# Local attention in blocks of 32 queries by 64 keys, in strips of TensorE, with two heads to a transpose and a bank for one head of two pairs

## The chip, the cores and the metric

The kernel runs on one core of a Trainium2 chip. The metric is the device time of one execution in microseconds (us). Five engines work side by side and meet at semaphores: TensorE (PE; its weight loads are shown apart as PEld), VectorE (DVE), ScalarE (ACT), GpSimd (POOL), and SyncE (SP), which here only issues DMAs. Matmul results land in PSUM, which has 8 banks of 128 partitions by 512 floats.

## The reference

Three layers follow each other on 4 sequences of 576 positions; 8 heads of 64 make a model width of 512.

```python
# q, k, v: (4, 8, 576, 64), float32
scores = scale * np.matmul(q, k.transpose(0, 1, 3, 2))
rel = pos[:, None] - pos[None, :]
mask_local = (rel >= 0) & (rel < 32)                                # heads 0 to 3
mask_strided = (rel >= 0) & (pos[None, :] % 32 == pos[:, None] % 32)  # heads 4 to 7
scores = np.where(masks, scores, -1e9)
attn = np.exp(scores - max); attn = attn / (sum + 1e-09); out = attn @ v
x = out as (2304, 512)
h = np.maximum(np.maximum(x @ w1, x @ w2), x @ w3); x = h @ w_out    # width 768
h = x @ w_in; g = np.maximum(h, 0) + alpha * np.minimum(h, 0); out = g @ w_out2  # width 2048
```

A query of a local head sees its own position and the 31 before it, so a block of 32 queries needs the 64 keys of its own block and of the block before.

## The kernel before

Every large product is split: a float32 number is held as two float32r parts (high and low), and three matmuls make the product. These matmuls leave one record in the trace each. The matmuls of the attention take plain float32 operands; each stands once in the program and leaves two records in the trace, a weight load and a matmul twice. A transpose (a matmul by the identity) leaves one.

The program has three stages. In the first, a planner (class Weave, lines 50 to 162) weaves together four kinds of tasks: the attention of all four sequences, the conversion of the weights (they arrive as float64 words; ACT and DVE make float32 of them, and cut that in two), the first layer's products for the first three sequences (gate_products, line 617; out1_products, line 639), and sums of weights for later. Each task has an engine, a cost in ns, a position that says how early it is wanted, and the tasks and buffers that it needs; the planner walks through time with these costs and writes down the order in which each engine gets its instructions. So the order is fixed when the kernel is built, and a change of a cost or a task moves others too. In the second stage the first layer runs for the last sequence, in the third the second layer runs for all (lines 1222, 1023 and 1029).

The attention is done in units: a sequence b, a pair of heads cc (0 and 1 are local, 2 and 3 strided; a pair lies in the 128 partitions of q and k, one head j in each 64), and a half hf of the sequence (288 positions). For a local unit there are 3 tiles of 96 queries by 128 keys, and for both heads:

- scores (line 331): 6 matmuls, each contracting 64 rows; head j writes its own bank.
- masked (line 339, DVE): adds the mask, scales, and takes the row minimum, per tile and head.
- exponential (line 346, ACT): exp with a row sum, per tile and head; then DVE takes reciprocals.
- normalise (line 368 on ACT or line 370 on DVE, as the planner chooses): per head, 3 tiles of 128 keys.
- transposes (line 378): 3 per head into a bank per head; keep (line 266 on ACT or DVE) copies the bank to a tile pt.
- values (line 403): 6 matmuls; head j writes 64 partitions of one bank; the result is split into x (a cast on ACT, a difference on DVE at line 269), the input of the first layer.

There are 16 local units, 4 per sequence, and 16 strided ones. The units of the first sequence come before any product can start; until then TensorE fills gaps with 38 matmuls whose results nobody reads (unread, line 215). A product of the first layer needs x of all four pairs of its half, and one converted weight tile. The weight tile's last two steps are a cast on ACT (line 266, "w<-word") and a difference on DVE (line 269, "w<-word,w").

```python
for i, (_, _, t, _) in enumerate(tiles):          # values, before
    for j in range(2):
        nc.tensor.matmul(pv[D * j:D * (j + 1), nq * i:nq * (i + 1)], v[:nk, t, j, :],
                         tl["pt", u, j][:nk, nq * i:nq * (i + 1)], start=True, stop=True)
```

Of the kernel before, what the change touches and what calls it, by code (L numbers as in the profile page):

```python
# [10 lines left out]
F32 = mybir.dt.float32  # L11
# [19 lines left out]
KT = 128  # L31
# [15 lines left out]
X_SPLIT = 10  # L47

# [117 lines left out]
def attention_maxout_prelu_kernel(  # L166
# [20 lines left out]
    mask_l = const.tile([QT, KT], F32, name="mask_l")  # L187
    mask_l0 = const.tile([QT, KT], F32, name="mask_l0")
# [3 lines left out]
    def build_constants():  # L192
# [4 lines left out]
        for m in (mask_l0, mask_l):  # L197
            g.memset(m, 0.0)
            g.affine_select(out=m, in_=m, compare_op=ALU.is_ge, fill=BIG, base=32,
                            pattern=[[-1, KT]], channel_multiplier=1)  # L200
            g.affine_select(out=m, in_=m, compare_op=ALU.is_ge, fill=BIG, base=-1,
                            pattern=[[1, KT]], channel_multiplier=-1)
        g.affine_select(out=mask_l0, in_=mask_l0, compare_op=ALU.is_ge, fill=BIG, base=-32,
                        pattern=[[1, KT]], channel_multiplier=0)
# [5 lines left out]
                        pattern=[[NA, 7], [0, NA]], channel_multiplier=-1)  # L210

# [35 lines left out]
    vp = pool(ax, "vp", 2)  # L247
# [13 lines left out]
    weave = Weave({"bank": 8, "q": 2, "third q": 1, "v": 2, "e": 3, "pt": 4, "x": 11, "t": 4, "h": 12,  # L261
# [19 lines left out]
    def geometry(cc, hf):  # L281

        if cc < 2:
            return QT, KT, [(QT * t, QT * t, t, mask_l0 if t == 0 else mask_l)
                            for t in range(3 * hf, 3 * hf + 3)]
# [6 lines left out]
    def load_task(b, cc, pos):  # L292
# [12 lines left out]
        def emit_v(_):  # L305
            v = tl[vk] = vp.tile([P, 6 if cc < 2 else 5, 2, D], F32, tag="v", name="v")
            nc.sync.dma_start(v, vl[b, cc] if cc < 2 else vs[b, cc - 2])

        add(load(592), emit_qk, pos, gives=[qk], makes=[("third q" if third else "q", qk)])
        add(load(350), emit_v, pos + 1, gives=[vk], makes=[("v", vk)])  # L310

    def attention_tasks(b, cc, hf, pos, step):
# [5 lines left out]
        ek, qk, vk = ("e", u), ("q", b, cc), ("v", b, cc)  # L318
        banks = [("sc", u, j) for j in range(2)]

        def scores(_):
# [3 lines left out]
            tl[ek] = ep.tile([P, 2, 3, KT], F32, tag="e", name="e")  # L325
            for name in ("nm", "sm", "rc"):
                tl[name, u] = smp.tile([P, 2, 3], F32, tag=name, name=name)
            for i, (qo, ko, _, _) in enumerate(tiles):
                for j in range(2):
                    rows = slice(D * j, D * (j + 1))  # L330
                    nc.tensor.matmul(sc[j][:nq, KT * i:KT * i + nk], q[rows, qo:qo + nq],  # L331
                                     k[rows, ko:ko + nk], start=True, stop=True)

        add((("PE", 2 * n * nk),), scores, pos, needs=[qk], gives=[("sc", u)],
            makes=[("bank", key) for key in banks] + [("e", ek)], uses=[qk], mode="scores")
        for i, (_, _, _, m) in enumerate(tiles):
            def masked(_, i=i, m=m):
                for j in range(2):
                    nc.vector.tensor_tensor_reduce(  # L339
                        out=tl[ek][:nq, j, i, :nk], in0=tl["sc", u][j][:nq, KT * i:KT * i + nk],  # L340
# [11 lines left out]
            add((("ACT", 750),), exponential, pos, needs=[("nm", u, i)], gives=[("exp", u)],  # L352
# [8 lines left out]
        for j in range(2):  # L361
            trk, ptk = ("tr", u, j), ("pt", u, j)

            def normalise(engine, j=j):
                e, rc = tl[ek][:nq, j, :n, :nk], tl["rc", u][:nq, j, :n]
                if engine == "ACT":
                    for i in range(n):
                        nc.scalar.activation(e[:, i], e[:, i], AF.Copy, scale=rc[:, i:i + 1])
                else:
                    nc.vector.tensor_tensor(out=e, in0=e, in1=rc.unsqueeze(2).to_broadcast([nq, n, nk]),  # L370
                                            op=ALU.mult)

            def transposes(_, j=j, trk=trk, ptk=ptk):
                tr = tl[trk] = bank()
                unread(tr, UNREAD.get((u, j), 0))
                tl[ptk] = ptp.tile([P, 3 * KT], F32, tag="pt", name="pt")
# [4 lines left out]
            def keep(e, trk=trk, ptk=ptk):  # L381
                copy(e, tl[ptk][:nk, :n * nq], tl[trk][:nk, :n * nq])

            add((dve(n * nk), ("ACT", n * (140 + 5 * nk // 6))), normalise, pos, needs=[("rc", u)],
                gives=[("nrm", u, j)], uses=[ek])
# [5 lines left out]
        pvk = ("pv", u)  # L391
        halves = [hf] if cc < 2 else [0, 1]
        xks = [("x", b, cc, h) for h in halves]
        fresh = [k for k in xks if k not in weave.users]

        def values(_):
# [3 lines left out]
            v = tl[vk]  # L400
# [7 lines left out]
            needs=[vk] + [("pt", u, j) for j in range(2)] + ([begun] if cc >= 2 and hf else []),  # L408
            gives=[pvk] + ([begun] if cc >= 2 and not hf else []), makes=[("bank", pvk)] + [("x", k) for k in fresh],
            uses=[vk] + [("pt", u, j) for j in range(2)] + xks, mode="values", slack=slack)  # L410

        def parts(h):
            x, pv = xt[b, cc, h], tl[pvk]
            if cc < 2:
                return x[:, 0, :], x[:, 1, :], pv[:, :n * nq]
# [5 lines left out]
        for h in halves:  # L421
            size = n * nq // len(halves)
            hik = ("xhi", u, h)
# [959 lines left out]
```

## Time and profile before

| | |
|---|---|
| median of 3 runs | 747.36 us (746.64 to 748.55) |
| the profiled execution | 747.21 us, of which its span from the first to the last instruction is 745.4 us |
| PE, PEld busy in the span | 99%, 96% |
| DVE, ACT, POOL busy | 85%, 64%, 4% |
| granted clock of TensorE | 1.000 |

A group line gives the busy time of all its instructions and the mean length of one, from start to end. Matmuls overlap each other, so on PE the length of one says little about the rate; the rate is read from a timeline, where one group's start can be set against the next group's start.

### The profile page before, as it was taken

Reading aid. Unit: us, or ns where it says so; the run is one execution under the profiler, and the core shown is the slowest. Engines: PE = TensorE matmul, PEld = TensorE weight load, DVE = VectorE, ACT = ScalarE, POOL = GpSimd, SP = SyncE. Lnnn points to the kernel's source line nnn. Section 1 sums busy time; section 2 is a strip of 40 time slices with the busy share of each in tenths; the row PEclk is TensorE's granted clock in tenths of the full one; section 3 lists DMA queues with packets and bytes.
Section 4 is the critical chain, followed back from the end, with each engine's and each line's share of the span. In section 5 each row is a group of like instructions: output and inputs, shape, how many; then the busy total and the mean of one; then the engine's idle time right before and its main releaser. Section 6 shows DMA issues by size and latency. Waiting matters only on the chain.

```text
span 745.4 us, 16034 instructions
## 1 busy us (share of the span) xinstructions
PE 736.9 (99%) x5586; PEld 712.7 (96%) x5586; DVE 629.9 (85%) x1684; ACT 475.2 (64%) x1268; POOL 27.6 (4%) x41
## 2 busy tenths in 40 slices
PE   9899999999999999999999999999999999999998
PEld 6699999999999999999999999999999999999997
DVE  5988998899989989558769898888989888988896
ACT  7997997779787677332255656624575654556571
POOL 1000000000000000034400000000000000000000
PEclk9999999999999999999999999999999999999999
DMA  8476779987999785579899789999788999877362
GB/s 302 132 231 211 252 257 318 357 313 267 316 323 352 266 271 201 172 278 336 279 323 389 270 296 333 381 397 384 250 306 302 365 402 370 284 240 265 107 200 75
DMA packets 88928, 211.95 MB, mean 284 GB/s; under 512 B 11024, under 2 KB 41232, under 8 KB 88848
## 3 DMA queue, kind: packets, MB, share of 16 engines
q1 hardware_dynamic: 88848, 210.94, 80.6%
q8 instruction: 44, 0.72, 0.4%
q14 instruction: 36, 0.29, 0.1%
HBM read 154.80 MB, written 56.10 MB: 283 GB/s over the span
## 4 chain that ended last, share of the span: by engine, by line
PE 89%; ACT 3%; DVE 3%; DMA 2%; POOL 2%; issue 1%; SPq 0%; POOLq 0%; ACTq 0%; DVEq 0%
PE bank L617 26%; PE ph L1222 22%; PE po L1023 15%; PE bank L639 10%; PE po L1029 4%; PE ph L1023 3%; PE bank L331 2%; PE bank L403 2%; PE bank L378 2%; PE po L1033 2%; ACT e L346 2%; POOL xst L223 1%; DMA xs<-x 1%; DMA xd<-xst 1%; PE bank L215 1%
## 5 line engine op out<-in xcount | busy, mean ns | idle before, releaser
L1222 PE MATMUL ph<-x,w 128*128 128x384 f32 x990 | 200.2, 337 | 0.2 <-DVE c L1228 0.2
L617 PE MATMUL bank<-x,w 128*128 128x288 f32 x1440 | 197.9, 296 | 1.2 <-DVE w L269 1.2
L617 PEld LDWEIGHTS bank<-x,w 128*128 128x128 f32 x1440 | 191.9, 188 | 3.3 <-DVE w L269 1.4
L1222 PEld LDWEIGHTS ph<-x,w 128*128 128x128 f32 x990 | 166.3, 188 | 1.4 <-DVE c L1228 0.7
L1023 PE MATMUL po<-w,g 128*128 128x256 f32 x936 | 135.6, 281 | 0.0
L1023 PEld LDWEIGHTS po<-w,g 128*128 128x128 f32 x936 | 130.1, 189 | 0.3
L1228 DVE TENSOR_TENSOR c<-ph,c 128x384 f32<-128x384 f32 x165 | 89.4, 554 | 30.3 <-PE ph L1222 27.5
L1016 ACT CAST g<-c 128x384 fp32r<-128x384 f32 x93 | 47.0, 506 | 91.1 <-DVE c L1206 51.7
L639 PE MATMUL bank<-h,w 128*128 128x288 f32 x576 | 79.8, 297 | 0.1
L639 PEld LDWEIGHTS bank<-h,w 128*128 128x128 f32 x576 | 76.9, 188 | 1.3 <-DVE h L777 0.4
L269 DVE TENSOR_TENSOR w<-word,w 128x512 fp32r<-128x512 f32 x100 | 63.4, 641 | 10.5 <-ACT w L266 9.8
L346 ACT ACTIVATE e<-e,nm 96x128 f32<-96x128 f32 (+2 forms) x176 | 68.2, 399 | 6.3 <-DVE nm L339 6.3
L1166 ACT ACTIVATE c<-c 128x384 f32<-128x384 f32 x96 | 50.5, 526 | 32.8 <-DVE c L1228 31.7
L266 ACT CAST w<-word 128x512 fp32r<-128x512 f32 x100 | 57.9, 590 | 12.7 <-DMA wh<-w 4.0
L1167 ACT ACTIVATE c<-c,nalpha 128x384 f32<-128x384 f32 x96 | 59.2, 617 | 3.1
L1171 DVE SCALAR_TENSOR_TENSOR c<-c 128x384 f32<-128x384 f32 x96 | 52.9, 551 | 6.4 <-ACT c L1167 6.4
L1017 DVE TENSOR_TENSOR g<-c,g 128x384 fp32r<-128x384 f32 x96 | 52.8, 550 | 0.9 <-ACT g L1016 0.5
L1017 DVE TENSOR_TENSOR g<-k,g 128x384 fp32r<-128x384 f32 x72 | 36.9, 550 | 7.5 <-ACT g L1016 7.5
L1029 PE MATMUL po<-w,g 128*128 128x512 f32 x120 | 43.0, 398 | 0.0
L469 ACT ACTIVATE word<-raw 128x512 f32<-128x512 f32 x56 | 37.4, 681 | 8.6 <-DMA raw<-in_w 5.0
L1206 DVE TENSOR_TENSOR k<-c 128x384 f32<-128x384 f32 x72 | 37.8, 550 | 0.0
L1016 ACT CAST g<-k 128x384 fp32r<-128x384 f32 x72 | 33.1, 514 | 7.1 <-PE ph L1023 3.3
(109 smaller groups left out, 953.2 us busy)
## 6 DMA issues: line engine op xcount, KB each, us to landing
w<-wh SPq DMA_DIRECT2D x72, 512.0 KB, 5.2
raw<-in_w SPq DMA_DIRECT2D x50, 512.0 KB, 4.8
w<-wo SPq DMA_DIRECT2D x48, 512.0 KB, 6.0
w<-wp SPq DMA_DIRECT2D x36, 512.0 KB, 6.2
wh<-w SPq DMA_DIRECT2D x24, 512.0 KB, 4.6
xd<-xst SPq DMA_DIRECT2D x28, 384.0 KB, 3.3
x<-xd SPq DMA_DIRECT2D x28, 384.0 KB, 8.4
ws<-w SPq DMA_DIRECT2D x12, 512.0 KB, 4.3
```

What stands on the lines that cost most here:

```text
L266: (nc.scalar.copy if e == "ACT" else nc.vector.tensor_copy)(out_, in_)
L269: nc.vector.tensor_tensor(out=out_, in0=x, in1=y, op=ALU.subtract)
L346: nc.scalar.activation(tl[ek][:nq, j, i, :nk], tl[ek][:nq, j, i, :nk], AF.Exp, bias=tl["nm", u][:nq, j, i:i + 1], scale=-1.0, accum_out=tl ...
L617: nc.tensor.matmul(acc, words["gate", f, g][:, wi, cc * P:(cc + 1) * P], xt[b, cc, hf][:, xi, :], start=n == 0, stop=n == 3 * NCC - 1)
L639: nc.tensor.matmul(acc, words["mix", f][:, wi, dc * P:(dc + 1) * P], st["h", hf, f][:, xi, :], start=n == 0, stop=n == 3 * NF1 - 1)
L1016: cast(g[:, 0], x)
L1017: return g, lambda: nc.vector.tensor_tensor(out=g[:, 1], in0=x, in1=g[:, 0].bitcast(F32), op=ALU.subtract)
L1023: nc.tensor.matmul(bank[:, NH * half:NH * (half + 1)], g[:, gi, t * P:(t + 1) * P], w[:, wi, off:off + NH], start=first and i == 0, stop=l ...
L1029: nc.tensor.matmul(bank.rearrange("p (s n) -> p s n", n=NH), g[:, 0, t * P:(t + 1) * P], w[:, :, off:off + NH], start=first, stop=last)
L1167: nc.scalar.activation(a, a, AF.Copy, scale=nalpha[:, f:f + 1])
L1222: nc.tensor.matmul(bank, words["h", n, i][:, wi, off + c * P:off + (c + 1) * P], x2h[blk, k, c][:, xi, :], start=m == 0, stop=m == 5)
L1228: nc.vector.tensor_tensor(out=out_, in0=bank, in1=other, op=ALU.add)
```

## The change

Local units are cut finer. Scores are made for 32 queries by 64 keys: 18 matmuls of 64 columns in a unit in place of 6 of 128, and a matmul's 64 contraction rows and 32 output partitions are those of one strip of TensorE out of six (two heads by three blocks of a tile). The mask and the tiles of scores and exponentials are 64 keys wide instead of 128. Both heads of a tile lie side by side in 128 columns, so normalise is one instruction for both heads on DVE alone, a transpose takes both heads (3 in a unit in place of 6), and one bank and one copy take what two did. The values of the two local pairs of a half are made in one task: 36 matmuls that contract 64 keys, with 64 output partitions and 32 columns, in four quadrants; a bank holds head j of both pairs. So x groups heads 0 and 2, and 1 and 3, and the rows of the first layer's weights are put in that order. The values' operand v is laid out by blocks of 64 keys, so that keys stand twice, and comes in one load per unit with 3 buffers instead of 2. The planner's costs for the new tasks are 500 and 1000 ns.

```diff
-KT = 128
+KW = 64
+NB = S // STRIDE
+COST = (500, 1000)
...
-        for m in (mask_l0, mask_l):
-            g.memset(m, 0.0)
-            g.affine_select(out=m, in_=m, compare_op=ALU.is_ge, fill=BIG, base=32,
-                            pattern=[[-1, KT]], channel_multiplier=1)
...
+        for m in (mask_l0, mask_l):
+            g.memset(m, 0.0)
+            for q in range(0, QT, STRIDE):
+                rows = m[q:q + STRIDE]
+                g.affine_select(out=rows, in_=rows, compare_op=ALU.is_ge, fill=BIG, base=STRIDE,
+                                pattern=[[-1, KW]], channel_multiplier=1)
+                g.affine_select(out=rows, in_=rows, compare_op=ALU.is_ge, fill=BIG, base=-1,
+                                pattern=[[1, KW]], channel_multiplier=-1)
...
-    vp = pool(ax, "vp", 2)
+    vp = pool(ax, "vp", 3)
...
+            if cc < 2:
+                for i, (qo, _, _, _) in enumerate(tiles):
+                    for o in range(0, QT, STRIDE):
+                        for j in range(2):
+                            rows = slice(D * j, D * (j + 1))
+                            nc.tensor.matmul(sc[j][o:o + STRIDE, KW * i:KW * (i + 1)],
+                                             q[rows, qo + o:qo + o + STRIDE],
+                                             k[rows, qo + o:qo + o + KW], start=True, stop=True)
+                return
...
-        add((("PE", 2 * n * nk),), scores, pos, needs=[qk], gives=[("sc", u)],
+        add((("PE", COST[0] if cc < 2 else 2 * n * nk),), scores, pos, needs=[qk], gives=[("sc", u)],
...
-        for j in range(2):
+        heads = [(0, 1)] if cc < 2 else [(0,), (1,)]
+        for js in heads:
...
+                elif len(js) == 2:
+                    nc.vector.tensor_tensor(out=e, in0=e, in1=rc.unsqueeze(3).to_broadcast([nq, 2, n, nk]),
+                                            op=ALU.mult)
...
                 for i in range(n):
-                    nc.tensor.transpose(tr[:nk, nq * i:nq * (i + 1)], tl[ek][:nq, j, i, :nk],
-                                        ident[:nq, :nq])
+                    e = (tl[ek][:nq, j, i, :nk] if len(js) == 1 else
+                         tl["whole e", u][:nq, rows * i:rows * (i + 1)])
+                    nc.tensor.transpose(tr[:rows, nq * i:nq * (i + 1)], e, ident[:nq, :nq])
...
+    def local_values(b, hf, pos, slack):
...
+            for t in range(NB // 2):
+                cols = slice(STRIDE * t, STRIDE * (t + 1))
+                for cc in range(2):
+                    for j in range(2):
+                        rows = slice(D * j, D * (j + 1))
+                        nc.tensor.matmul(tl[pvs[j]][D * cc:D * (cc + 1), cols],
+                                         tl[vks[cc]][rows, D * t:D * (t + 1)], tl[pts[cc]][rows, cols],
+                                         start=True, stop=True)
+
+        add((("PE", COST[1]),), values, pos, needs=vks + pts, gives=pvs,
...
+            if cc < 2:
+                values_task(("v", b, cc, hf), vl[b, cc, hf], first + step * i - 7)
...
-    vl = np.stack([vpad[:, :, QT * t:QT * t + KT] for t in range(6)], axis=2)
+    vl = np.stack([vpad[:, :, STRIDE * t:STRIDE * t + KW] for t in range(NB)], axis=3)
...
+    w1 = np.stack([moe_w1, moe_w2, moe_w3]).reshape(3, H, D, F1)[:, [0, 2, 1, 3, 4, 5, 6, 7]]
```

The order of PE's instructions in the second sequence's attention, among the first sequence's products (L617 and L639 before, L682 and L704 after). Before, from a group of transposes to the values of the sequence's last local units:

```order
L378 MATMUL bank<-ident,e 128x96 x6
L331 MATMUL bank<-k,q 96x128 x6
L639 MATMUL bank<-h,w 128x288 x36
L617 MATMUL bank<-x,w 128x288 x36
L331 MATMUL bank<-k,q 108x108 x6
L403 MATMUL bank<-pt,v 64x96 x12
L378 MATMUL bank<-ident,e 128x96 x12
L639 MATMUL bank<-h,w 128x288 x18
L403 MATMUL bank<-pt,v 64x96 x12
```

The same place in the changed kernel (L346 are the local scores, L408 the transposes, L483 the local values):

```order
L408 MATMUL bank<-ident,e 128x96 x3
L346 MATMUL bank<-k,q 32x64 x18
L704 MATMUL bank<-h,w 128x288 x18
L408 MATMUL bank<-ident,e 128x96 x3
L704 MATMUL bank<-h,w 128x288 x18
L682 MATMUL bank<-x,w 128x288 x36
L408 MATMUL bank<-ident,e 128x96 x3
L483 MATMUL bank<-pt,v 64x32 x36
```

Six score matmuls have become 18, six transposes three, and twelve value matmuls 36; they still stand between products.

PE's order where the first products begin, at the end of the first sequence's attention. Before:

```order
L378 MATMUL bank<-ident,e 128x96 x6
L331 MATMUL bank<-k,q 96x128 x6
L403 MATMUL bank<-pt,v 64x96 x6
L215 MATMUL bank<-warm_r 128x512 x9
L378 MATMUL bank<-ident,e 128x96 x6
L331 MATMUL bank<-k,q 108x108 x6
L403 MATMUL bank<-pt,v 64x96 x6
L378 MATMUL bank<-ident,e 128x96 x6
L331 MATMUL bank<-k,q 126x126 x4
L403 MATMUL bank<-pt,v 64x96 x6
L617 MATMUL bank<-x,w 128x288 x240
```

After, from the same 9 unread matmuls:

```order
L218 MATMUL bank<-warm_r 128x512 x9
L408 MATMUL bank<-ident,e 128x96 x3
L353 MATMUL bank<-k,q 108x108 x6
L483 MATMUL bank<-pt,v 64x32 x36
L408 MATMUL bank<-ident,e 128x96 x3
L353 MATMUL bank<-k,q 126x126 x4
L682 MATMUL bank<-x,w 128x288 x12
L408 MATMUL bank<-ident,e 128x96 x3
L682 MATMUL bank<-x,w 128x288 x12
L483 MATMUL bank<-pt,v 64x32 x36
L682 MATMUL bank<-x,w 128x288 x216
```

Two products (12 matmuls each) now stand ahead of the second half's values, where all of them stood behind.

ACT's order in the same stretch, from the last exponentials of the first sequence's local units to the third cast of a weight ("w<-word"). Before:

```order
L266 COPY pt<-bank 128x288
L368 ACTIVATE e<-e,rc 96x128 x3
L478 ACTIVATE raw<-raw 128x512
L266 CAST x<-bank 128x288
L266 COPY pt<-bank 128x288 x2
L469 ACTIVATE word<-raw 128x512
L346 ACTIVATE e,sm<-e,nm 108x108 x2
L266 CAST x<-bank 128x288
L266 COPY pt<-bank 128x288
L346 ACTIVATE e,sm<-e,nm 108x108 x2
L478 ACTIVATE raw<-raw 128x512
L266 CAST w<-word 128x512
```

After, from the copy of the first local unit's transposes (L368 are the exponentials here, L534 and L543 steps of the weights' conversion):

```order
L269 COPY pt<-bank 128x288
L368 ACTIVATE e,sm<-e,nm 96x64 x4
L269 CAST w<-word 128x512
L368 ACTIVATE e,sm<-e,nm 96x64 x6
L269 CAST w<-word 128x512
L269 CAST x<-bank 128x288 x2
L269 COPY pt<-bank 128x288
L534 ACTIVATE word<-raw 128x512 x3
L543 ACTIVATE raw<-raw 128x512 x3
L269 COPY pt<-bank 128x288
L769 COPY t<-bank 128x288
L269 CAST w<-word 128x512 x3
```

The first weight cast has moved ahead of the last local exponentials and the second right behind them; the exponentials of the next sequence's strided units (108x108) have moved behind five casts; the normalise on ACT is gone. Before, three instructions stand between the first and the second cast (two exponentials among them), and six exponentials between the second and the third.

## Rows read from the trace of the kernel before

**Rows 1.** The page: span, busy time of PE, clock in 40 slices (tenths).

```profile
span 745.4 us, 16034 instructions
PE   9899999999999999999999999999999999999998
PEclk9999999999999999999999999999999999999999
```

**Rows 2.** Busy time of each engine (instructions) in two stretches, clock, DMA share, GB/s.

```profile
20.00:37.00 17.00, 14.13 (x156) 10.50 (x152) 15.62 (x89) 17.00 (x74) 0.00 (x0) 1.00 0.44 138
37.00:313.00 276.00, 276.00 (x2355) 267.03 (x2356) 244.18 (x748) 217.71 (x661) 0.00 (x0) 1.00 0.81 276
```

**Rows 3.** The chain that ended last: the piece that follows the first stretch.

```profile
36.99 31.79 PE bank L617 x238
```

**Rows 4.** PE's timeline around a local unit's scores: start, length, records.

```profile
89.30 0.90 PE L331 MATMUL bank<-k,q 64*96 64x128 f32 x12
90.13 0.78 PE L403 MATMUL bank<-pt,v 108*64 108x108 f32 x12
```

**Rows 5.** PE's timeline: values and transposes of two local units, then products.

```profile
114.98 1.21 PE L403 MATMUL bank<-pt,v 128*64 128x96 f32 x24
116.12 1.21 PE L378 MATMUL bank<-ident,e 96*128 96x96 f32 x12
117.12 2.66 PE L639 MATMUL bank<-h,w 128*128 128x288 f32 x18
```

**Rows 6.** Weight loads by shape over the run: busy, mean ns of one.

```profile
L617 PEld LDWEIGHTS bank<-x,w 128*128 128x128 f32 x1440 | 191.9, 188 | 3.3 <-DVE w L269 1.4
...
L403 PEld LDWEIGHTS bank<-pt,v 128*64 128x64 f32 x192 | 8.8, 136 | 2.3 <-ACT pt L266 1.0 <-issue 0.7
```

**Rows 7.** PE's timeline where the first products begin.

```profile
34.41 0.95 PE L403 MATMUL bank<-pt,v 128*64 128x96 f32 x12
35.29 0.53 PE L617 MATMUL bank<-x,w 128*128 128x288 f32 x2
36.99 3.23 PE L617 MATMUL bank<-x,w 128*128 128x288 f32 x22 [1.17 <-DVE w L269]
```

**Rows 8.** ACT's timeline before and at the first weight casts.

```profile
29.11 0.99 ACT L368 ACTIVATE e<-e,rc 96x128 f32<-96x128 f32 x3
30.00 0.67 ACT L478 ACTIVATE raw<-raw 128x512 uint32<-128x512 uint8 x1
...
34.62 0.62 ACT L266 CAST w<-word 128x512 fp32r<-128x512 f32 x1
...
38.96 0.62 ACT L266 CAST w<-word 128x512 fp32r<-128x512 f32 x1
```

**Rows 9.** Groups of ACT and DVE by shape over the run: busy, mean ns.

```profile
L346 ACT ACTIVATE e<-e,nm 96x128 f32<-96x128 f32 x96 | 37.7, 405 | 1.8 <-DVE nm L339 1.8
...
L346 ACT ACTIVATE e<-e,nm 108x108 f32<-108x108 f32 x48 | 18.0, 384 | 4.5 <-DVE nm L339 4.5
...
L368 ACT ACTIVATE e<-e,rc 96x128 f32<-96x128 f32 x36 | 11.9, 405 | 0.6 <-DVE rc L358 0.6
...
L266 ACT COPY pt<-bank 128x288 f32<-128x288 f32 x29 | 10.0, 411 | 0.0
...
L339 DVE CUSTOM_DVE_ANT_0 e<-bank,mask_l 96x128 f32<-96x128 f32 x96 | 21.4, 282 | 0.5 <-PE bank L331 0.4
...
L339 DVE CUSTOM_DVE_ANT_0 e<-bank,mask_s 108x108 f32<-108x108 f32 x48 | 9.7, 264 | 6.0 <-PE bank L331 6.0
...
L370 DVE TENSOR_TENSOR e<-e,rc 96x384 f32<-96x384 f32 x20 | 10.6, 547 | 0.0
```

**Rows 10.** POOL's groups: one of the mask's instructions, busy, mean ns.

```profile
L199 POOL TENSOR_SCALAR_AFFINE_SELECT mask_l<-mask_l 96x128 f32<-96x128 f32 x2 | 0.6, 289 | 0.1
```

**Rows 11.** DVE's timeline: the first use of a local mask.

```profile
15.53 0.28 DVE L339 CUSTOM_DVE_ANT_0 e<-bank,mask_l 96x128 f32<-96x128 f32 x1
```

**Rows 12.** DMA issues: number, KB each, median us to landing.

```profile
v<-in_vl SPq DMA_DIRECT2D x8, 384.0 KB, 3.8
```

More of the change, by code (lines that the diff above doesn't have):

```diff
@@ L283, in geometry @@
         if cc < 2:
[L284 removed]
+            return QT, KW, [(QT * t, QT * t, t, mask_l0 if t == 0 else mask_l)
                             for t in range(3 * hf, 3 * hf + 3)]
@@ L303, in emit_qk, with values_task, emit @@
             tl[qk] = q, k
-        def emit_v(_):
-            v = tl[vk] = vp.tile([P, 6 if cc < 2 else 5, 2, D], F32, tag="v", name="v")
-            nc.sync.dma_start(v, vl[b, cc] if cc < 2 else vs[b, cc - 2])
         add(load(592), emit_qk, pos, gives=[qk], makes=[("third q" if third else "q", qk)])
-        add(load(350), emit_v, pos + 1, gives=[vk], makes=[("v", vk)])
+        if cc >= 2:
+            values_task(vk, vs[b, cc - 2], pos + 1)
+    def values_task(vk, src, pos):
+        def emit(_):
+            tl[vk] = vp.tile([P, 10 * D], F32, tag="v", name="v")
+            n = src.shape[1]
+            nc.sync.dma_start(tl[vk][:, :n], src)
+        add(load(src.shape[1] // 2), emit, pos, gives=[vk], makes=[("v", vk)])
     def attention_tasks(b, cc, hf, pos, step):
@@ L351, in attention_tasks @@
                 uses=banks + [ek])
-            add((("ACT", 750),), exponential, pos, needs=[("nm", u, i)], gives=[("exp", u)],
+            add((("ACT", 640 if cc < 2 else 750),), exponential, pos, needs=[("nm", u, i)], gives=[("exp", u)],
                 uses=[ek])
@@ L374, in transposes @@
+            def transposes(_, j=j, js=js, trk=trk, ptk=ptk):
                 tr = tl[trk] = bank()
                 unread(tr, UNREAD.get((u, j), 0))
-                tl[ptk] = ptp.tile([P, 3 * KT], F32, tag="pt", name="pt")
+                tl[ptk] = ptp.tile([P, 3 * P], F32, tag="pt", name="pt")
+                rows = nk * len(js)
                 for i in range(n):
-                    nc.tensor.transpose(tr[:nk, nq * i:nq * (i + 1)], tl[ek][:nq, j, i, :nk],
-                                        ident[:nq, :nq])
@@ L386, in attention_tasks, with keep @@
+            def keep(e, js=js, trk=trk, ptk=ptk):
+                rows = nk * len(js)
+                copy(e, tl[ptk][:rows, :n * nq], tl[trk][:rows, :n * nq])
+            add((dve(n * nk * len(js)),) + ((("ACT", n * (140 + 5 * nk // 6)),) if len(js) == 1 else ()),
+                normalise, pos, needs=[("rc", u)], gives=[("nrm", u, j)], uses=[ek])
             add((("PE", 95 * n),), transposes, pos + step, needs=[("nrm", u, j)], gives=[trk],
@@ L389, in attention_tasks @@
                 uses=[trk, ptk])
-        pvk = ("pv", u)
-        halves = [hf] if cc < 2 else [0, 1]
-        xks = [("x", b, cc, h) for h in halves]
+        pts = [("pt", u, js[0]) for js in heads]
+        if cc < 2:
+            if cc == 1:
+                local_values(b, hf, pos + 2 * step, slack)
+            return
+        vk, pvk = ("v", b, cc), ("pv", u)
+        xks = [("x", b, cc, h) for h in (0, 1)]
         fresh = [k for k in xks if k not in weave.users]
@@ L407, in attention_tasks @@
         add((("PE", 2 * n * 85),), values, pos + 2 * step,
-            needs=[vk] + [("pt", u, j) for j in range(2)] + ([begun] if cc >= 2 and hf else []),
-            gives=[pvk] + ([begun] if cc >= 2 and not hf else []), makes=[("bank", pvk)] + [("x", k) for k in fresh],
-            uses=[vk] + [("pt", u, j) for j in range(2)] + xks, mode="values", slack=slack)
+            needs=[vk] + pts + ([begun] if hf else []),
+            gives=[pvk] + ([] if hf else [begun]), makes=[("bank", pvk)] + [("x", k) for k in fresh],
+            uses=[vk] + pts + xks, mode="values", slack=slack)
         def parts(h):
             x, pv = xt[b, cc, h], tl[pvk]
-            if cc < 2:
-                return x[:, 0, :], x[:, 1, :], pv[:, :n * nq]
             r0, nr = RG[tiles[0][2]][0], n * nq // NA
```

74 lines of the change are left out of this document (43 added, 31 removed).

## The prediction

> **What bounds the kernel now.** I read the page first: PE is busy in nearly every slice, and its granted clock is at full speed (2.4 GHz) throughout [rows 1]. Then the stretches: from 37 to 313 us, where the attention of the last three sequences is woven between the first layer's products, PE is busy for all of 276 us, DVE for 244 and ACT for 218 [rows 2]. There PE's own time is the time, and what comes off PE comes off the run. From 20 to 37 us it is ACT that never rests (17.00 of 17.00), while PE has 14.13 busy, part of it matmuls that nobody reads [rows 2]. The chain agrees: from 36.99 us it is PE alone, 238 products in a row [rows 3]. The first product starts at 35.29, waits for a weight's low part from DVE, and PE runs without a gap from 36.99 [rows 7]. So two things can be gained: PE time behind 37 us (12 local units, 6 pairs of them), and an earlier start, which ACT and DVE decide.
>
> **How long local attention takes on PE now.** Starts are compared, since lengths overlap. Scores of a unit: 12 records from 89.30 to 90.13, 0.83 us [rows 4]. Values of two units: 24 records from 114.98 to 116.12, 1.14 us; transposes of two units: 12 records from 116.12 to 117.12, 83 ns each [rows 5]. A transpose passes 96 columns and fills the array: 83 ns is twice 96 columns at 2.4 GHz (80 ns) and 3 ns. A value record passes 96 columns too, but they come every 47.5 ns, although each must last as long: two run side by side, one in each half of the columns. Twelve rounds of 83 ns are 0.99 us, the other 0.15 us goes at the change of shapes. Scores likewise: 128 columns are 107+3 ns, six rounds of two make 0.66, and 0.17 goes at the ends. So I take as rule, from these rows, that a plain float32 record of n columns holds its own strip for 2n/2.4+3 ns, and that different strips work side by side.
>
> The Trainium skill says that tiles of the array load weights and multiply independently, and lists eight of 64x32 and four of 64x64 (TensorEngine Tiling (Array Packing), Tiling Modes). The two-strip rows agree; no row shows more than two at a time.
>
> **The change on PE.** Scores: 36 records of 64 columns in six strips, six rounds of 56 ns, with 0.17 at the ends 0.51 us; I take 0.53, since the last strip of a round starts later. That is 0.30 less a unit, 3.6 us for 12. Transposes: three of 83 ns less, 0.25 a unit, 3.0 us. Values: 72 records of 32 columns in four quadrants, 18 rounds. The columns take 27+3 ns, but each record first needs 64 weight columns: a load of 128 columns takes 188 ns and one of 64 takes 136 [rows 6], so 64 columns cost 52 ns beyond a fixed part. I take 55 ns, 18 rounds 0.99, with the ends 1.14: no gain. (At 30 ns a round, 0.69: another 2.7 us off; that is the bound below.) Sum behind 37 us: 6.6 us. A bound above comes from the fastest rate that a row shows, 47.5 ns from record to record [rows 5]: with s ns between records, twelve times (36s+0.17-0.83 us), six times (72s+0.15-1.14 us) and the transposes' 3.0 make 864s-16.9 us, so -16.9 is what it takes off and s decides. Rounds of 56 for six and 55 for four strips are a mean s of 12. At 47.5 ns it would be 24 us more, at 19.5 ns nothing. I take the side of the concurrent strips, since the rows show the second strip of a pair costing next to nothing.
>
> **The change on ACT and DVE, in the first stretch.** An exponential of 128 columns takes 405 ns and one of 108 takes 384, so 1.05 ns a column: 64 columns less are 67 ns, 24 of them in the first sequence 1.6 us. The three normalise instructions on ACT, 0.99 us there [rows 8], are gone, and five copies of 411 ns (about 0.3 from start to start) become three [rows 9]. That is 3.2 us off an engine that was full. On DVE the mask drops by 0.9 ns a column (282 against 264 ns), 58 ns by 24, 1.4 us; seven normalise instructions (547 ns each; eight heads less the one that ACT did) become four of the same 384 elements, 1.6 us [rows 9]. Beside this the order on ACT changes. Before the third weight cast, which ended at 39.58 [rows 8], stood 12 exponentials of the next sequence's strided units; they go behind it (12 by 0.37 from start to start, 4.4 us), and five more conversion steps come ahead of it (0.67 long [rows 8], about 0.58 from start to start, 2.9 us). With the 3.2 us and 0.5 of small copies that go to DVE or behind, the third cast ends near 39.6-3.2-4.4+2.9-0.5 = 34.4. Products were in step with it before: one takes 12x31.79/238 = 1.60 us [rows 3], so the third was due at 40.2, just behind cast and difference. Now the first two products can start near 30.5, when the pair's x is done, and the third near 35.0. The delayed exponentials come back ahead of the sixth weight: its cast I count at 40.5 and its product from 41.2 to 42.8, against 36.99+6x1.60 = 46.6. I take 3.8 us, with 2 to 6.5 as bounds: 2 where little more than half of the 3.2 us that ACT sheds arrives, 6.5 where products start at 30.5 and never wait.
>
> **What costs nothing.** GpSimd makes 12 selects for the local masks instead of 5; at 289 ns each [rows 10] it is 2 us later, and DVE first reads a local mask at 15.53 us [rows 11], long behind it. Without that cover it would delay the first local unit by 2 us. Values come in 16 loads of 288 KB in place of 8 of 384 [rows 12], 1.5 MB more; in the stretch from 37 us the DMA engines have 19% free at 276 GB/s [rows 2], and 1.5 MB takes some 6 us of 276. One of these loads now stands on SP's queue ahead of the first weight loads; 288 KB is about 1 us at that rate, and the first cast (34.62 [rows 8]) waits for ACT, not for its load. With three buffers in place of two, loads wait less for a free one, and the weights behind them on the queue too. The weights' row order moves no instruction.
>
> **Sum.** The profiled execution took 747.21 us, 1.8 more than its span, and is within 0.2 of the median. 747.2-6.6-3.8 = **736.8 us**. Its own range is 731 to 742: at one end 2.7 us more off in the values and 6.5 at the start, at the other 2 at the start and half of PE's gain.
>
> **Rivals.**
> - *Only two strips at a time* (slower). Whatever lets two records run may not hold six. Then scores take 18 rounds of 56 ns, 1.18 us, and values 36 of 55, 2.13: 12x0.35+6x0.99-3.0 = 7.1 us more; the start keeps some 2 us: 752. For it: no row shows three. Against it: rows show both ways of cutting the array, by rows (scores) and by columns (values), each at work. It decides as soon as the mean spacing is over 24 ns (864s = 16.9+3.8 with the start's gain).
> - *A floor under the spacing of records*, whatever their strips. For it: 47.5 ns is the closest mean that a timeline row has. At 24 ns it just cancels all gains, at 30 it is 5 us slower. Against it: in these rows columns explain the whole time. I price it where it about cancels: 748.
> The Trainium skill states such a floor: start to start never below 25 ns however few the columns (TensorE: Matmul & The Clock Gate, "Wait — 56ns, not 53.3ns?"), and warns against tiling a dimension that is already small (TensorEngine Tiling (Array Packing), Instruction Overhead). If it held across strips, 864x25 ns gives 21.6-16.9 = 4.7 us more on PE, and 748.1 in all. The trace neither bears it out nor refutes it: its closest mean is 47.5 ns.
> - *The strips do not work side by side at all* (the change doesn't do what it says): 36 records at 56 ns are 2.2 us, 72 at 55 are 4.1: 12x1.35+6x3.0-3.0 = 31 us more, 778. Against it: the pairs in today's rows.
> - *The start gives nothing*, since DVE, 15.6 of 17 us busy, holds back the weights: 740.6, still faster.
>
> **How the numbers follow.** Change in both parts as worked out (731 to 742): 0.70, of which the start without gain has 0.08 at its upper end. Two strips at a time 0.09; a floor or slow issue near 748 0.10; no concurrency 0.03; a new wait that I don't see, with a small change either way, 0.08. From no change the runs can tell about 0.3%, 2.2 us: faster (under 745.1) 0.74, same 0.11, slower 0.15. The range of 8 in 10 must take in the rival near 748: 729.5 to 750.
>
> **What would show it.** Six strips: the timeline has 36 records of local scores in about 0.5 us, and 72 of values in about 1.1. If scores take 1.1 or more, one of the slow rivals is right; the values tell which (1.8 times the scores' length for two at a time, twice for a floor). Transposes stand three at a time, 0.25 us. The first products start near 30 us, with a pause before the third, and PE has no gap from about 35. In the stretch to the last product of the first stage, which ended at 313, PE stays full, and the next stage starts 11 us earlier. The forecast is wrong if PE shows gaps behind the start that end on DVE's normalise (now on DVE alone), or if its clock drops in the first stretch, where PE now has less to do.

## The result, and the profile after

The changed kernel takes 738.7 us (median of 4 executions, 737.37 to 738.95) against 747.16 beside it: a ratio of 0.988 (95% interval 0.9862 to 0.9898), 8.5 us faster, where 10.4 were forecast. The profiled execution took 737.37 us, 735.5 of it span, so 9.8 us less than that of before.

The page of the changed kernel: span, PE's share in 40 slices, and its clock in tenths.

```profile
span 735.5 us, 17464 instructions
...
PE   8899999999999999999999999999999999999998
...
PEclk9999999999999999999999999999999999999999
```

Of the 40 slices only the first (18 us) shows PE less full than before [rows 1]. The stretches say where the time came from. First the changed kernel, cut at its first product, the end of its sixth product, the end of its 138th product (114 of 12 matmuls and 24 of 18), and the first product of the last stage; columns as in [rows 2].

```profile
0.00:30.60 30.60, 25.88 (x383) 19.90 (x383) 20.61 (x142) 24.66 (x113) 4.67 (x24) 1.00 0.74 254
30.60:42.50 11.90, 11.59 (x149) 11.05 (x148) 11.27 (x32) 11.90 (x36) 0.00 (x0) 1.00 0.93 315
42.50:313.70 271.20, 271.20 (x2910) 262.83 (x2909) 235.00 (x748) 197.82 (x607) 0.00 (x0) 1.00 0.81 278
313.70:375.90 62.20, 62.20 (x470) 62.20 (x469) 49.41 (x105) 24.92 (x62) 22.80 (x22) 1.00 0.92 331
```

Before, cut at the same places of the program:

```profile
0.00:35.20 35.20, 31.66 (x290) 23.50 (x290) 25.99 (x158) 30.04 (x131) 3.23 (x16) 1.00 0.61 215
35.20:46.40 11.20, 10.03 (x75) 9.71 (x73) 10.06 (x34) 10.83 (x40) 0.00 (x0) 1.00 0.75 249
46.40:322.40 276.00, 276.00 (x2358) 267.03 (x2357) 240.71 (x739) 211.98 (x638) 0.00 (x0) 1.00 0.81 276
322.40:385.00 62.60, 62.45 (x470) 62.22 (x469) 45.13 (x97) 21.57 (x54) 22.63 (x22) 1.00 0.84 299
```

Up to the end of the sixth product the changed kernel gains 46.40-42.55 = 3.85 us. In the long stretch, where PE is busy for the whole of it in both kernels, it gains 4.85 (276.03 and 271.18 between single records), with 552 more PE records. The remaining 1.1 us lie in the two later stages, whose work has not changed; in the profiles of the other runs the last stage alone takes from 359.5 to 361.2 us, so this part is not shown to come from the change (it took 360.3 before and 359.6 here).

PE's timeline where the local units' work stands between products (start, length, records), answering [rows 4, 5]:

```profile
89.39 0.62 PE L346 MATMUL bank<-k,q 64*32 64x64 f32 x36
89.94 0.78 PE L437 MATMUL bank<-pt,v 108*64 108x108 f32 x12
...
109.93 0.41 PE L408 MATMUL bank<-ident,e 96*128 96x96 f32 x3
110.27 1.25 PE L483 MATMUL bank<-pt,v 64*64 64x32 f32 x72
111.46 1.28 PE L353 MATMUL bank<-k,q 64*108 64x108 f32 x20
```

36 score records take 0.55 us from start to start where 12 took 0.83, and 72 value records take 1.19 where 24 took 1.14. That is 15.3 and 16.5 ns from record to record. Read record by record (a finer reading than these merged lines), starts in different strips stand 6.5 ns apart, the six of a scores' round come again after 56 ns, the four of a values' round after 58.

PE's timeline in the head, answering [rows 7]:

```profile
16.92 0.49 PE L408 MATMUL bank<-ident,e 108*108 108x108 f32 x3 [1.69 <-DVE e L397]
...
24.22 0.44 PE L408 MATMUL bank<-ident,e 96*128 96x96 f32 x3 [1.76 <-DVE e L394]
...
30.64 1.85 PE L682 MATMUL bank<-x,w 128*128 128x288 f32 x12
32.80 0.47 PE L408 MATMUL bank<-ident,e 96*128 96x96 f32 x3 [0.31 <-DVE e L394]
33.04 1.94 PE L682 MATMUL bank<-x,w 128*128 128x288 f32 x12
34.91 1.25 PE L483 MATMUL bank<-pt,v 64*64 64x32 f32 x72
```

The first products start at 30.64 and 33.04, the third at 36.09, right behind the values, and from 33.04 on PE has no gap. Further up it now stands idle twice for 1.7 us, behind DVE's normalise (the experiments come back to this). ACT's timeline in the head, the weights' casts, answering [rows 8]:

```profile
26.34 0.61 ACT L269 CAST w<-word 128x512 fp32r<-128x512 f32 x1
...
28.86 0.61 ACT L269 CAST w<-word 128x512 fp32r<-128x512 f32 x1
...
34.57 1.70 ACT L269 CAST w<-word 128x512 fp32r<-128x512 f32 x3
```

ACT's group of local exponentials over the run, answering [rows 9]:

```profile
L368 ACT ACTIVATE e<-e,nm 96x64 f32<-96x64 f32 x96 | 32.7, 353 | 0.7 <-DVE nm L361 0.6
```

DVE's groups of local masks, and of normalise for both heads:

```profile
L361 DVE CUSTOM_DVE_ANT_0 e<-bank,mask_l 96x64 f32<-96x64 f32 x96 | 15.0, 215 | 1.0 <-PE bank L346 0.9
...
L394 DVE TENSOR_TENSOR e<-e,rc 96x384 f32<-96x384 f32 x16 | 8.8, 548 | 0.1
```

Weight loads of the local values and scores, answering [rows 6]:

```profile
L483 PEld LDWEIGHTS bank<-pt,v 64*64 64x64 f32 x576 | 9.1, 135 | 1.1 <-issue 0.5 <-DVE rc L380 0.2 <-ACT t L769 0.2
L346 PEld LDWEIGHTS bank<-k,q 64*32 64x32 f32 x576 | 7.4, 106 | 2.4 <-issue 0.7 <-PE bank L408 0.5 <-ACT e L368 0.2
```

An exponential is 52 ns shorter than one of 128 columns and a mask 67 ns; 16 normalise instructions are left. 32 weight columns load in 106 ns, 64 in 135.

### The profile page after: what moved, and what is told of

It reads as the page before. It is cut to its first block, busy times and chain, and to the rows that moved or that the text cites. A ratio compares the mean times of both kernels' runs of the same rounds, so it can differ in the third digit from the quotient of the medians.

```text
span 735.5 us, 17464 instructions
## 1 busy us (share of the span) xinstructions
PE 727.1 (99%) x6306; PEld 706.1 (96%) x6306; DVE 623.0 (85%) x1680; ACT 459.1 (62%) x1221; POOL 29.2 (4%) x49
## 4 chain that ended last, share of the span: by engine, by line
PE 96%; DVE 2%; ACT 1%; POOL 1%; issue 0%; POOLq 0%
PE bank L682 26%; PE ph L1289 24%; PE po L1090 15%; PE bank L704 11%; PE bank L855 5%; PE po L1096 4%; PE ph L1090 4%; PE po L1100 2%; PE bank L408 2%; PE bank L483 1%; PE bank L437 1%; PE bank L346 1%; PE bank L353 1%; ACT e L368 1%; DVE e L361 1%; PE bank L218 1%
## 5 line engine op out<-in xcount | busy, mean ns | idle before, releaser
L682 PE MATMUL bank<-x,w 128*128 128x288 f32 x1440 | 198.5, 296 | 0.0
L682 PEld LDWEIGHTS bank<-x,w 128*128 128x128 f32 x1440 | 191.9, 188 | 1.6 <-issue 0.2
L704 PE MATMUL bank<-h,w 128*128 128x288 f32 x576 | 79.7, 297 | 0.0
L704 PEld LDWEIGHTS bank<-h,w 128*128 128x128 f32 x576 | 76.8, 188 | 0.6
L368 ACT ACTIVATE e<-e,nm 96x64 f32<-96x64 f32 (+2 forms) x176 | 63.5, 372 | 5.5 <-DVE nm L361 5.2
L772 DVE TENSOR_TENSOR t<-bank,t 128x288 f32<-128x288 f32 x72 | 32.7, 454 | 12.8 <-PE bank L682 8.9
L534 ACT ACTIVATE word<-raw 128x512 f32<-128x512 f32 x56 | 37.2, 683 | 8.5 <-DMA raw<-in_w 4.8
```

The source lines that it names most:

```text
L368: nc.scalar.activation(tl[ek][:nq, j, i, :nk], tl[ek][:nq, j, i, :nk], AF.Exp, bias=tl["nm", u][:nq, j, i:i + 1], scale=-1.0, accum_out=tl ...
L682: nc.tensor.matmul(acc, words["gate", f, g][:, wi, cc * P:(cc + 1) * P], xt[b, cc, hf][:, xi, :], start=n == 0, stop=n == 3 * NCC - 1)
L704: nc.tensor.matmul(acc, words["mix", f][:, wi, dc * P:(dc + 1) * P], st["h", hf, f][:, xi, :], start=n == 0, stop=n == 3 * NF1 - 1)
```

## The experiments

The theory behind the forecast: different strips of the array really work side by side, the loads of 64 weight columns set the values' rounds, and the earlier start comes from the work that ACT sheds. The rivals: concurrency that is only partial, columns (or issue) that set the values' rounds, and a start that is earlier only because the planner, fed other costs, wrote another order.

**The order of the strips.** In the changed kernel six matmuls in a row go to six strips. Here the loops are turned, so that six in a row go to only two strips by turns (one block of queries, both heads):

```diff
-                for i, (qo, _, _, _) in enumerate(tiles):
-                    for o in range(0, QT, STRIDE):
+                for o in range(0, QT, STRIDE):
+                    for i, (qo, _, _, _) in enumerate(tiles):
```

> The same 18 score matmuls of a local unit, but the three tiles stand inside the loop over the blocks of 32, so that the next matmul but one is in the same strip again and six in a row use only two strips. Theory A (a strip's records wait in a short line of their own, and the matmuls behind them wait too): two strips work at a time, 18 rounds of 56 ns, so a unit's scores go from 0.55 us to about 1.15, and the run gets 12 x 0.6 = 7 us longer (746). Theory B (TensorE looks far enough ahead to find the other strips itself): scores stay at 0.55 us and the time at 738.7.

It took 741.57 us (741.18 to 742.06), a ratio of 0.9916 (0.9902 to 0.9931). PE's timeline of this kernel, a unit's scores:

```profile
90.70 0.82 PE L346 MATMUL bank<-k,q 64*32 64x64 f32 x36
91.45 0.78 PE L437 MATMUL bank<-pt,v 108*64 108x108 f32 x12
```

0.75 us a unit, 20.9 ns from record to record: between the two theories. Two strips kept busy would need 1.15, and if the order played no part it would be 0.55. So PE does reach past a busy strip, but not far enough to fill all six. Twelve units by 0.20 are 2.4 us in the long stretch; the run is 2.9 us longer than the changed kernel's. The two don't cover each other exactly: in its profile the long stretch is 3.9 us longer, and the other 1.5 us lie on products, 0.54 of them in two waits for weights at 44 and 45 us.

**What sets the values' round.** Half the weight columns (32 of 64; ahead of them one wide matmul of a constant, not shown here, fills each bank, so half of each head's values is left out), and, in another kernel, double the moving columns (64 instead of 32; a later block overwrites the surplus, and the last block also part of the one before it, so two blocks of values are not the reference's):

```diff
...
-                        nc.tensor.matmul(tl[pvs[j]][D * cc:D * (cc + 1), cols],
-                                         tl[vks[cc]][rows, D * t:D * (t + 1)], tl[pts[cc]][rows, cols],
+                        nc.tensor.matmul(tl[pvs[j]][D * cc:D * cc + 32, cols],
+                                         tl[vks[cc]][rows, D * t:D * t + 32], tl[pts[cc]][rows, cols],
```

> The local values load 32 weight columns instead of 64 (half of each head's 64 value columns is left out; a matmul of 288 columns ahead fills the bank so that the rest can be read). 72 records as before. Theory A (a round of four value records takes as long as loading 64 weight columns): a round falls from 58 ns to about 32, the 72 records from 1.18 us to about 0.7; the filling matmul adds about 0.3 us a pair, so the run is some 6 x 0.2 = 1 us shorter. Theory B (records cannot start closer than 14.6 ns on average): the 72 records stay near 1.15 us and the run is 2 us longer.

```diff
-                cols = slice(STRIDE * t, STRIDE * (t + 1))
+                c0 = min(STRIDE * t, HALF - 64)
+                cols = slice(c0, c0 + 64)
```

> The local values pass 64 columns in each matmul instead of 32 (each block's columns and the next block's, so later matmuls write over part of it; the results are not the reference's values). Theory A (columns pass while the next weights load, and the longer of the two counts, 52 against 53 ns): the 72 records stay at 1.18 to 1.25 us and the run within 0.5 us of 738.7. Theory C (loading weights and passing columns add up in a strip): a round grows by 27 ns, 18 rounds by 0.48 us, the run by about 3 us.

PE's timeline with 32 weight columns, a pair's values and what follows:

```profile
111.29 0.82 PE L485 MATMUL bank<-pt,v 64*32 64x32 f32 x72
112.04 1.28 PE L353 MATMUL bank<-k,q 64*108 64x108 f32 x20
```

And with 64 moving columns:

```profile
112.26 1.28 PE L484 MATMUL bank<-pt,v 64*64 64x64 f32 x72
113.47 1.28 PE L353 MATMUL bank<-k,q 64*108 64x108 f32 x20
```

Half the weight columns take the pair from 1.19 to 0.75 us (10.6 ns from record to record as mean of the long stretch's six pairs, rounds of 32 to 33). Twice the moving columns change it by 0.02, to 1.21. So 64 weight columns cost about 58 ns a round and 64 moving columns fit beneath them: 32 moving columns take as long as 64. That it is the load, and not something else that goes with the number of weight columns, is argued from sizes: a load shrinks from 135 to 106 ns as mean of one, 29 ns, and the round by 26. The whole runs took 737.99 (737.46 to 742.13) and 740.11 us (738.5 to 743.12), 0.988 (0.9853 to 0.9908) and 0.9906 (0.9877 to 0.9935); they spread more than this difference (the second had a granted clock below 1.000 in all four executions, and missed the range expected for the run), and the timelines carry the verdict.

**ACT's shed work put back.** Twelve copies of 256 columns that nobody reads, after the exponentials of the first sequence's local units:

```diff
+                if b == 0 and cc < 2:
+                    nc.scalar.copy(tl["whole e", u][:nq, 384:640].rearrange("p (s n) -> p s n", n=P),
+                                   ident[:nq].unsqueeze(1).to_broadcast([nq, 2, P]))
```

> The changed kernel, with 12 copies of 256 columns added on ScalarE behind the exponentials of the first sequence's local units (results that nobody reads), about 3.2 us in all, in the same order otherwise. Theory A (the first products begin earlier because ScalarE sheds 3.2 us ahead of them): the sixth product ends 2.5 to 3.2 us later than 42.5 us, and the run takes about 741.5. Theory B (the earlier beginning comes from the other order alone, or VectorE sets it): the sixth product ends within 1 us of 42.5, and the run stays at 738.7.

It took 741.41 us (740.98 to 743.08), 0.9918 (0.9903 to 0.9933); the two executions at a clock of 1.000 took 740.98 and 741.0. PE's timeline of its head:

```profile
31.03 0.53 PE L685 MATMUL bank<-x,w 128*128 128x288 f32 x2
32.50 1.59 PE L685 MATMUL bank<-x,w 128*128 128x288 f32 x10 [0.93 <-DVE w L272]
34.77 0.47 PE L411 MATMUL bank<-ident,e 96*128 96x96 f32 x3 [0.68 <-DVE e L397]
35.02 1.95 PE L685 MATMUL bank<-x,w 128*128 128x288 f32 x12
```

The wait of the first product for a weight's low part is back (0.93, where [rows 7] show 1.17). The third product starts at 38.08, and the sixth ends at 44.62, 2.07 us later than in the changed kernel. The copies are 0.41 to 0.45 us long each and 0.30 from start to start, 3.6 us in all, and they delay the sixth product by less than the 2.5 to 3.2 us expected. So about half of the 3.85 us gained in the head goes with what ACT sheds; how the rest divides, this run doesn't show. (In the profiled execution PE also waited at the last stage's start; the head lies ahead of it.)

**The planner's costs.** The tasks' costs as they were in sum before, and, in another kernel, as measured here:

```diff
-COST = (500, 1000)
+COST = (768, 1020)      # one kernel
+COST = (550, 1180)      # the other
```

> The planner counts local scores and values as long as before the change (768 and 1020 ns in place of 500 and 1000), so only the order of instructions differs from the changed kernel. Theory A (the gain comes from shorter work on TensorE and from work that ScalarE and VectorE shed; the order follows): within 1.5 us of the changed kernel. Theory B (the order that the new costs bring is what makes the early beginning): the sixth product ends 2 us or more later than 42.5 us, and the run is 2 to 4 us longer.

> The planner counts local scores and values as measured (550 and 1180 ns). Theory A: within 1.5 us of the changed kernel, either way. Theory B (the order decides): a difference of 2 us or more.

The first took 740.33 us (738.06 to 743.16), 0.9909 (0.9887 to 0.993), the second 737.01 (736.25 to 741.83), 0.9855 (0.9841 to 0.9869). The changed kernel beside them took 738.02. By the run alone the first is 2.3 us longer, as theory B had it; but three of its six executions have a lower clock (741.78 to 743.16), and the three at 0.999 or more took 738.06 to 738.89. PE's timeline of its profile, at full clock:

```profile
15.41 0.49 PE L408 MATMUL bank<-ident,e 108*108 108x108 f32 x3
...
26.14 0.44 PE L408 MATMUL bank<-ident,e 96*128 96x96 f32 x3 [1.54 <-DVE rc L379]
...
34.25 11.97 PE L682 MATMUL bank<-x,w 128*128 128x288 f32 x84
```

The sixth product (the 60th of these 84 matmuls ends it) is done at 42.85 and the 138th at 313.82, both within 0.3 us of the changed kernel. This order also has eight of the next sequence's strided exponentials ahead of ACT's third weight cast again, which starts at 36.37 instead of 34.57. So neither these two costs nor the place of those exponentials is what brings the start. Not tested is an order that follows from the rest of the change: the planner has fewer tasks, and counts a local exponential at 640 ns instead of 750. The measured costs give executions down to 736.25, but one of 741.83, and that leads to the next question.

**The spread.** Both kernels of the last pair have executions at 740 us and more, and in each of those the mean granted clock is 0.993 to 0.998 instead of 1.000. The changed kernel was run twice more, beside this pair and beside a later kernel.

> The changed kernel as it is, as a measure for the three others on the same chip: 738 to 739 us. Its first sequence leaves TensorE idle twice for 1.7 us; where the clock falls after that, the first products begin later.

> The changed kernel again, as a measure for the next on the same chip: 737.5 to 739 us.

738.02 us (737.26 to 739.53), 0.9879 (0.9865 to 0.9893), and 740.04 (737.25 to 742.4), 0.989 (0.9869 to 0.9912); the second lies outside what was expected. Of 14 executions of the changed kernel in all, the 8 at a clock of 1.000 took 737.25 to 738.81, the 6 below it 738.95 to 742.4. A lower clock doesn't cost time everywhere, though. The kernel before, run beside these series, has a mean clock of 0.993 to 0.995 in 3 of 29 executions, and their times (747.62 to 749.09) lie within those of the others (746.42 to 749.14); with the turned loops, executions at 0.997 and 0.998 took 741.18 to 742.06, and the one at 1.000 took 741.85. The profile of the last series fell on the one of 742.4; its PE timeline:

```profile
17.31 0.78 PE L408 MATMUL bank<-ident,e 108*108 108x108 f32 x3 [1.69 <-DVE e L397]
17.78 3.23 PE L218 MATMUL bank<-warm_r 128*128 128x512 f32 x7
...
20.84 0.44 PE L408 MATMUL bank<-ident,e 108*108 108x108 f32 x3
...
26.17 0.44 PE L408 MATMUL bank<-ident,e 96*128 96x96 f32 x3 [1.76 <-DVE e L394]
26.55 0.62 PE L346 MATMUL bank<-k,q 64*32 64x64 f32 x36
27.10 3.83 PE L218 MATMUL bank<-warm_r 128*128 128x512 f32 x9
```

Its windows over the two groups of unread matmuls (the clock stands third from the end):

```profile
17.50:20.50 3.00, 3.00 (x10) 2.42 (x10) 1.19 (x5) 3.00 (x11) 0.00 (x0) 0.50 0.75 237
...
27.50:30.50 3.00, 3.00 (x9) 2.32 (x8) 1.55 (x15) 3.00 (x18) 0.00 (x0) 0.51 0.89 280
```

Behind each of the two idle stretches the granted clock is at its lower level (1.2 GHz), and seven unread matmuls take 3.06 us from start to start, where they take 1.71 (17.18 to 18.89 in the profile at full clock). The first product comes at 34.16 instead of 30.64, the sixth ends at 46.09 instead of 42.55. Not all of the 5.0 us between the two executions is the clock's: 0.4 of these 3.5 stands ahead of the first fall (17.31 against 16.92), the long stretch takes 271.18 us in both, and 1.5 us lie in the two later stages, at full clock. The same two gaps stand in the profile at full clock, so a gap is not always followed by the fall. In the kernel with the measured costs the lower level reached into the products (PE's timeline):

```profile
25.86 0.44 PE L408 MATMUL bank<-ident,e 96*128 96x96 f32 x3 [1.35 <-DVE rc L379]
...
33.12 3.25 PE L682 MATMUL bank<-x,w 128*128 128x288 f32 x12
```

There twelve matmuls of a product take 3.25 us (1.85 above). Two kernels fill the gaps with matmuls that nobody reads, one with the changed kernel's costs and one with the measured costs:

```diff
-UNREAD = {(0, 3, 0): 6, ((0, 2, 0), 0): 8, ((0, 3, 0), 1): 7, ((0, 1, 0), 0): 9}
+UNREAD = {(0, 3, 0): 6, ((0, 2, 0), 0): 8, ((0, 3, 0), 1): 7, ((0, 1, 0), 0): 9,
+          ((0, 3, 0), 0): 6, ((0, 0, 0), 0): 7}                                          # one kernel
+UNREAD = {(0, 3, 0): 6, ((0, 2, 0), 0): 8, ((0, 3, 0), 1): 7, ((0, 1, 0), 0): 14}        # the other
```

> 13 more matmuls that nobody reads fill TensorE's two idle stretches of 1.7 us in the first sequence (6 and 7 of about 0.235 us). Theory A (the idle stretches let the clock fall in some executions, and that delays the first products by up to 2 us): no execution shows a lower clock before 40 us, the times lie closer together and the median is 0 to 1 us below the changed kernel. Theory B (the first products wait for weights, whatever the clock did): the same median as the changed kernel, or up to 1 us more, where the filling stands in the way.

> The costs as measured (550 and 1180 ns), and 14 instead of 9 matmuls that nobody reads ahead of one group of transposes (1.2 us more), where the kernel with these costs left TensorE idle for 1.35 us and its profiled execution had a lower clock for 10 us. Theory A (the clock makes the slow executions of that kernel): all executions between 736 and 737.5 us, the third product near 34.3 us, faster than the changed kernel by 1 to 2 us. Theory B (the slow executions have another cause): some still take 740 us or more.

They took 738.39 us (737.86 to 738.57), 0.988 (0.9867 to 0.9893), and 737.48 (736.46 to 738.66), 0.9866 (0.9852 to 0.988). PE's timeline of the first of them, at the two places where the gaps were:

```profile
15.17 1.66 PE L219 MATMUL bank<-warm_r 128*128 128x512 f32 x6
...
22.39 1.88 PE L219 MATMUL bank<-warm_r 128*128 128x512 f32 x7
```

In none of the 8 executions did the clock fall below 0.999, and their longest is 738.66. Four of each are few: if 6 in 14 fall, four in a row without a fall come about once in nine tries ((8/14) to the fourth), so that the fill prevents it is likely, not shown. At full clock the fill gains nothing: the sixth product ends at 42.52, as without it. The range expected of the second, 736 to 737.5, was missed by two of its four. The second of the two has a lower median than the changed kernel beside it (740.04) and than before (747.57). What it may have over the changed kernel is steadiness: at a clock of 1.000 the changed kernel took 737.25 and 737.33 there, inside its range.

## Why the prediction was right, point by point

**What bounds.** Right: PE is full from 33.04 us (36.99 before) to the end of the first stage, and time off PE came off the run.

**Scores.** 0.53 us a unit were forecast, 0.55 came, and the rule behind it held: a strip is held for its columns, and other strips work beside it. Over the long stretch, 12 units went from 9.79 us to 6.65 (-3.1, where -3.6 was forecast; the unit that I read before took 0.83, the mean was 0.82). The turned loops add what the forecast didn't consider: the order of the strips counts, because PE reaches only some way past a busy one.

**Transposes.** Right: 72 records with 6.02 us became 36 with 3.14, -2.9 against -3.0.

**Values.** The mechanism was right (weight loads, not columns), the round 58 ns instead of 55: 6.85 us became 7.09, +0.2 against 0.

**The rivals on PE.** All of them needed a mean spacing of at least about 24 ns over the 864 records; it is 15.9 (13.74 us by 864). The Trainium skill's 25 ns from start to start (TensorE: Matmul & The Clock Gate, "Wait — 56ns, not 53.3ns?") does not hold from strip to strip: with half the weight columns the mean is 10.6.

**The head.** The gain was 3.85 where 3.8 were forecast, with its steps in place: first product 30.64 (30.5 forecast), sixth ended at 42.55 (42.8). The third started at 36.09, not 35.0: its cast, among three from 34.57 on, ended some 0.7 us later than the 34.4 forecast, and a pair's values stand on PE until 36.09. The pause before it, which I had put down to the cast, is filled by these values. That 3.85 meets 3.8 so closely is in part luck. An exponential shed 52 ns, not 67, which is 0.4 us less over 24, and the third product came 1.1 us late. The term for the exponentials that move behind the cast (4.4 us) was not needed: with the costs of before eight of them stand ahead of it again, and the sixth product ends only 0.30 us later.

**The sum.** The mis-sized term is "Sum behind 37 us: 6.6 us"; the long stretch gained 4.85. Scores were 0.5 short, values and transposes 0.4. Another 0.6 is a step left out of the sum: 12 more strided score records (60 instead of 48, 3.48 us instead of 2.91) now run behind the sixth product. I had seen on ACT that their exponentials move behind the casts, but charged nothing for their scores on PE, which move with them. So part of the head's gain is only moved. With the costs of before they stand ahead again (48 behind): there the long stretch gains 5.06 and the head 3.55. The last 0.4 us are spread over records that did not change (products +0.2). Of the 9.8 us between the two profiled executions, 1.1 lie in the later stages, for which the forecast had no term: what it did forecast came to 8.7 of 10.4.

**The condition named for a miss** came about: gaps behind DVE's normalise, and a clock below 1.000 in 6 of 14 executions (in the two of these that were profiled the fall lies in the first stretch). Four of the six are in its third series, whose median stood at 740 us. But only the second gap stands behind a normalise of a local unit. The first stands behind one of a strided unit, whose work has not changed. DVE's timeline before, and in the changed kernel:

```profile
14.08 0.49 DVE L370 TENSOR_TENSOR e<-e,rc 108x324 f32<-108x324 f32 x1
```

```profile
16.38 0.48 DVE L397 TENSOR_TENSOR e<-e,rc 108x324 f32<-108x324 f32 x1
```

The reciprocals that it needs end at 14.04 before and at 14.07 in the changed kernel, where DVE then makes six local masks and a difference of x first. With the costs of before it starts at 14.35, ahead of the masks, and this gap is gone (the row at 15.41 above waits for nothing). So the first gap comes from the order that the two new costs bring. I had costed normalise by its length alone, and not asked where it stands in DVE's order and what PE does in the meantime.

**What cost nothing.** DVE's first local mask stood at 15.53 before and at 14.76 after; the 16 loads left the DMA engines at 0.81 in the long stretch, as before. Neither showed a price in this kernel. In the last of the kernels above PE waited 0.74 us for one of these loads (its values at 32.79).

## What to carry to other kernels

Where a matmul fills a corner of the array, cut it so that neighbours in program order go to different strips; price it, as the two shapes here suggest, as the larger of its columns and of the load of its weight columns, by the longest chain in one strip, and not by its number of instructions. Take a profile of the first, lightly loaded microseconds too: an instruction that moves to another engine, or to another place in its order, can leave PE idle there, and what follows is then paid in some executions and not in others. When a median moves by less than the spread, compare executions at the same granted clock first.

## What the runs showed of the hardware that was not expected

- Six strips work at once, with starts 6.5 ns apart and 15.3 ns a record as mean of a unit; ordered badly, the same records take 20.9 ns.
- In the profiles, idle stretches of PE of 1.35 to 1.77 us in the first 27 us were followed in some executions by some 3 to 10 us at 1.2 GHz, in others (1.31 to 1.76 us) by none. Once this came much later: in the kernel with the twelve copies PE waited 1.94 us at the last stage's start (a row of its timeline), and the clock was at the lower level behind it.

```profile
380.10 3.81 PE L1292 MATMUL ph<-x,w 128*128 128x384 f32 x12 [1.94 <-ACT xo L914]
```

- Why the same gap has this effect in some executions only stays open; filling it was tried, in eight executions, and no other remedy.
